# Parity of a position as an outer index, and transform tables from phases on TensorE

## The chip, the cores and the metric

One core of a Trainium2 chip runs the whole kernel. The metric is the device time of one execution in microseconds. Engines are named as in the profile: PE (TensorE), PEld (its weight loads), ACT (ScalarE), DVE (VectorE), POOL (GpSimd) and SP (SyncE, which here issues transfers). Each engine works through its own list of instructions in order; semaphores order the engines against each other.

## The reference

A state-space layer and a gated feed-forward block on the same normalised input, and all gradients of their combination. L = 2048 positions, D = 576 channels, N = 128 states, F = 4608 hidden units; inputs and outputs are bf16.

```python
def A(u):                                     # state-space layer
    dt = exp(log_dt)[:, None]
    P = exp((dt * (A_re + 1j * A_im))[:, :, None] * arange(L))
    K = einsum("dn,dnl,dn->dl", C_re + 1j * C_im, P, dt * (B_re + 1j * B_im)).real
    y = irfft(rfft(pad(u, L)) * rfft(pad(K, L)))[:L]          # causal convolution
    return y + u * Dskip
def B(x):                                     # feed-forward
    return (silu(x @ w1) * (x @ w3)) @ w2
xn = layernorm(u)
out = u + A(xn) * silu(B(xn))
# returned: out, and the vjp with grad_out for u, A_re, A_im, B_re, B_im, C_re, C_im,
# log_dt, Dskip, w1, w3, w2
```

## The kernel before, in words

The work runs in stages that overlap, each a Python generator whose steps a planner places by the times that the code gives (`self.at(...)`), with a few explicit orders (`issue_after`). The times below are those of the profile.

*Front (0 to 101 us).* The parameters are loaded, and DVE builds products of `dt` with A's parts, split into bf16 pieces `pc` that go through `PCS_dram` (L463) into the matmul operand `lhs_r`. POOL builds with iota instructions (in `selector_values`, L522) the rows `sel_dl` and `sel_val`. `early_exps` then forms on PE (through a helper, so that its line is L637) the exponents, and ACT takes 54 exponentials `E_k` of 128x1024, stored to `E_dram`. Some of these matmuls (`odd`) are followed by a second one over every other column, which adds what belongs to the odd positions. In between the layer norm (`stats`, `xn_bf`, on DVE) is computed, its transposes `xnT`, and from the normalised input and the transform's table `cCS` the early spectrum `u_e`, stored to `UH_dram` by POOL (L657). POOL also computes the products `Wr`, `Wi` of B and C.

*Kernel generation (about 101 to 340 us).* A position is l = 64a + b. The 32 values of a are split into parts whose innermost is, before the change, the parity. For each of 36 chunks of 16 channels, `kgen_chunk` takes phases on PE from `lhs_t` and the selectors `SEL` into `et_ps` (L711), their sines on ACT (`cs_k`, L713, read as 16-bit integers, so that whole turns fall off), and products with the loaded exponentials `E_l` on DVE: `p_k` (L719, stored to `PZ_dram` by SP at L722) and `q_k` (L723, to `Q_dram` at L727). `kgen_sum` multiplies `v_k` and `q_k` on PE into `kps` (L749), and POOL lays the result into the kernel's tile `KT` (L758). Between these instructions stand the matmuls of the feed-forward's hidden part (`pg`, `pu`, L1040 and L1048, with weights `wmB_w`), whose results ACT and DVE take out as `s_t`, `u_t` and `g_t` (L1058). SP also issues the loads of `E_l` (L690) and the stores of `h_t` (L1065).

At chunks 16 and 24 `dft_kernel_half` makes one half each of the tables `fT` of the kernel's transform: columns `dft_tk` on DVE, products with the row of frequencies on POOL (L812), reduction to a turn on DVE (L782 to L784), and a sine and a cosine on ACT (L816, L819), with DVE between (L817). At chunk 32 `conv_loads` stores `fT` to `TF_dram`, and SP issues eight DMA transposes of it into `iT`, the table of the inverse transform in the backward pass.

*Forward convolution and feed-forward (about 334 to 700 us).* `conv_half` transforms blocks of `KT` (`dft_block`), multiplies them with the loaded spectra and goes back. It is called for two halves of the channels.

*Backward (700 to 1731 us).* `conv_bwd_quarter`, for four quarters of the channels and up to about 1064 us, gives the gradient by the kernel and by the convolution's input. The former comes from `idft_pair` on PE (L873, with `iT`) as two position tiles at a time in `et_ps`, which ACT writes into `gk_st` with three instructions: L1341 both tiles at once, L1344 twice, scaled by the position (`lcol`). In `gk_st` the tile index t of 16 is innermost, so the two tiles t and t+1 of L1341 lie side by side (2 bytes each) and the next channel follows 32 bytes on; L1344 writes one tile. Beside this run the feed-forward's gradients (`ph` L1762, `gh` L1765, `pgw` and `gw` L1803 to L1828). Then follow the sums for the parameters (L1392 to L1400, which load `gz` from `gK_dram`) and the input gradient (`px`, L1875).

Of the kernel before, what the change touches and what calls it, by code (L numbers as in the profile page):

```python
# [10 lines left out]
ACT = mybir.ActivationFunctionType  # L11
ALU = mybir.AluOpType
AX = mybir.AxisListType
FP32 = mybir.dt.float32
BF16 = mybir.dt.bfloat16
I32 = mybir.dt.int32
I16 = mybir.dt.int16
P = 128
# [82 lines left out]
class K:  # L101
# [410 lines left out]
    def selector_values(self, st):  # L512
        nc, cfg = self.nc, self.cfg
        AV, BV, DC = cfg.AV, cfg.BV, 16
        QW, PW = DC * BV, DC * AV
        self.sel_pi = st.tile([P, 1], I32, name="pi_")
        nc.gpsimd.iota(self.sel_pi[:], pattern=[[1, 1]], base=0, channel_multiplier=1)
        self.sel_dl = dl = st.tile([P, QW + 2 * PW], BF16, name="sel_dl")
        self.sel_val = val = st.tile([P, QW + 2 * PW], BF16, name="sel_val")

        def io(out, pattern):
            nc.gpsimd.iota(out, pattern=pattern, base=0, channel_multiplier=0, allow_small_or_imprecise_dtypes=True)  # L522

        io(dl[:, 0:QW], [[1, DC], [0, BV]])
        io(val[:, 0:QW], [[0, DC], [2, BV]])
        o = QW + PW
        for k in range(2):
            io(dl[:, QW + k * PW:o + k * PW], [[4, 4], [1, 2], [2, 2], [0, AV]])
        io(val[:, QW:o], [[0, DC], [2 * BV, 2], [4 * BV, AV // 4], [0, 2]])
        io(val[0:64, o:o + PW], [[0, DC], [0, 2], [0, AV // 4], [1, 2]])  # L530
        io(val[64:P, o:o + PW], [[0, DC], [2, 2], [4, AV // 4], [0, 2]])
        return val

    def selector_rows(self, st):
# [52 lines left out]
    def conv_loads(self, after, part):  # L587
        nc, cfg = self.nc, self.cfg
        sync = Chain(self.tc, nc.sync)
        sync.prev = after  # L590
        if part == 0:
            self.skip_row = self.matp.tile([1, cfg.D], BF16, name="skip_row")
            with nc.allow_non_contiguous_dma(reason="small vector load"):
                sync.dma_start(out=self.skip_row[:].rearrange("p (g h d) -> p g h d", g=4, h=2),
                               in_=self.aps["A_Dskip"].rearrange("(o h g d) -> o g h d", o=1, h=2, g=4))
            self.CS_dram = self.dram.tile([2, 2, P, cfg.LS], BF16, name="CS_dram")
            sync.dma_start(out=self.CS_dram[:].rearrange("m i p k -> p m i k"), in_=self.cCS[:])
        elif part == 1:
            self.cT = self.matp.tile([P, 2, cfg.KT, 2 * P], BF16, name="cT")
            for m in range(2):  # L600
                for i in range(2):
                    sync.dma_start_transpose(out=self.cT[:, m, :, i * P:(i + 1) * P], in_=self.CS_dram[m, i])
        else:
            self.TF_dram = self.dram.tile([P, 2, 4, 2 * P], BF16, name="TF_dram")
            sync.dma_start(out=self.TF_dram[:], in_=self.fT[:])
            self.iT = self.matp.tile([P, 2, 2, 4, P], BF16, name="iT")
            for m in range(2):
                for i in range(4):
                    sync.dma_start_transpose(out=self.iT[:, m, :, i], in_=self.TF_dram[:, m, i])

    def early_exps(self, SELR, LR_, ep, ps):
        nc, cfg = self.nc, self.cfg
        DC = 16
        NCH = cfg.D // DC
        TW = DC * (cfg.AV + cfg.BV)
        self.e_stores, self.e_lead = [], None
        self.E_dram = self.dram.tile([NCH // 2, P, 2 * TW], BF16, name="E_dram")
        for n in range(3 * NCH // 2):
            c2, o = 2 * (n // 3), 1024 * (n % 3)
            E = ep.tile([P, 1152], BF16, name="E_k")  # L620
            self.pre(14 + 0.95 * n)
            pe = ps.tile([P, 1024], FP32, name="e_ps")
            for k in (0, 1) if n >= self.TURN else (0, 0, 1):
                ch, o1 = divmod(o + 512 * k, TW)
                odd = o1 == DC * cfg.BV
                self.lead(nc.tensor.matmul, pe[:, 512 * k:512 * k + 512], lhsT=LR_[:, c2 + ch, :], rhs=SELR[:, o1:o1 + 512],
                          start=True, stop=not odd)
                if odd:
                    self.lead(nc.tensor.matmul, pe[:, 512 * k + 1:512 * k + 512:2], lhsT=LR_[:, c2 + ch, :],
                              rhs=SELR[:, TW + 1:TW + 512:2], start=False, stop=True)  # L630
            self.S.activation(out=E[:, 0:1024], in_=pe[:], func=ACT.Exp)
            self.e_stores.append(nc.sync.dma_start(out=self.E_dram[c2 // 2, :, o:o + 1024], in_=E[:, 0:1024]))
            yield
# [25 lines left out]
    def ssm_kernel(self, T0, TK, ps, ps1):  # L659
        nc, cfg = self.nc, self.cfg  # L660
        D, N = cfg.D, cfg.N
        AV, BV = cfg.AV, cfg.BV
        DC = 16
        NCH = D // DC
        TW = DC * (AV + BV)
        GE = 6
        assert NCH % GE == 0 and AV == 2 * cfg.LT
        with self.pool(name="kg_l", bufs=2) as lp, \
# [6 lines left out]
            for ch in range(NCH):  # L675
                yield T0 + TK * ch
                self.at(T0 + TK * ch)
                if ch in (16, 24):
                    self.dft_kernel_half(dp, (ch - 16) // 8, T0 + TK * ch, TK)
                    self.at(T0 + TK * ch)  # L680
                if ch % GE == 0:
                    LT_ = lp.tile([P, GE, N], BF16, name="lhs_t")
                    nc.gpsimd.memset(LT_[:], 1.0)
# [4 lines left out]
                                                  "(k p) n -> p k n", p=DC))  # L688
                E = ep.tile([P, TW], BF16, name="E_l")
                el = self.kg_load = nc.sync.dma_start(out=E[:], in_=self.E_dram[ch // 2, :, ch % 2 * TW:(ch % 2 + 1) * TW])  # L690
                if ch in (8, 18, 32):
                    self.conv_loads(el, (8, 18, 32).index(ch))
                qv = self.kgen_chunk(ch, E, LT_[:, ch % GE, :], self.SEL, sb, qvp, ps)
                prev.append(qv)
                if ch >= 2:
# [100 lines left out]
    def dft_sines(self):  # L796
        self.turn_sines(self.S, self.cCS[:, 1], self.cCS[:, 0], self.dft_fr, self.dft_q)

    def dft_kernel_half(self, sb, i, T, TK):
        nc = self.nc  # L800
        if i == 0:
            self.fT = self.matp.tile([P, 2, 4, 2 * P], BF16, name="fT")
        sl = slice(2 * i, 2 * i + 2)
        t = sb.tile([P, 2], FP32, name="dft_tk")
        fr = sb.tile([P, 2, 2 * P], FP32, name="dft_frk")
        q = sb.tile([P, 2, 2 * P], FP32, name="dft_qk")
        for r in range(2):
            with self.tc.issue_after(self.v_last.ins):
                nc.vector.tensor_scalar(out=t[:, r:r + 1], in0=self.pcol[:], scalar1=2.0, scalar2=float(256 * i + r), op0=ALU.mult,
                                        op1=ALU.add)  # L810
        for r in range(2):
            nc.gpsimd.tensor_scalar(out=fr[:, r], in0=self.frow[:, 0:2 * P], scalar1=t[:, r:r + 1], scalar2=None, op0=ALU.mult)  # L812
        self.at(T + 0.5 * TK)
        self.wrap_turns(nc.vector, fr, q, 4.0 * self.cfg.LS)
        self.at(T + 1.5 * TK)
        nc.scalar.activation(out=self.fT[:, 1, sl], in_=fr[:], func=ACT.Sin, scale=-6.283184)  # L816
        nc.vector.scalar_tensor_tensor(out=q[:], in0=fr[:], scalar=-1.0, in1=fr[:], op0=ALU.mult, op1=ALU.max)  # L817
        self.at(T + 2.5 * TK)
        nc.scalar.activation(out=self.fT[:, 0, sl], in_=q[:], func=ACT.Sin, scale=-6.283184, bias=self.halfpi_col[:])  # L819

    def dpieces(self):
        D = self.cfg.D
# [93 lines left out]
    def conv_half(self, h, T0, TC, kp, up, rp, ypool, tp, spool, epool, ps):  # L916
# [10 lines left out]
        for b in range(NB):  # L927
            self.at(T0 + TC * 4.5 * b)
            k2 = kp.tile([P, 2, 2, KT, HW], BF16, name=f"k2_{b}")
            kr = rp.tile([P, 2, 2, KT, HW], BF16, name="kraw") if b else k2  # L930
            self.dft_block(ps, epool, lambda tt: self.KT[:, b * KT + tt, cs], kr)
            self.marks.append(self.dft_last)
            if b:
                self.shifted(k2, kr, prev, 0)
# [1 line left out]
            nc.sync.dma_start(out=self.KH2_dram[2 * h:2 * h + 2, b].rearrange("q p r k d -> p q (r k d)"),  # L936
                              in_=k2[:].rearrange("p q r k d -> p q (r k d)"))
            K2.append(k2)
        for m in range(NB):
            self.at(T0 + TC * (18, 28, 43, 65)[m])  # L940
            u = up.tile([P, 2, 2, KT, HW], BF16, name=f"u_{m}")
# [261 lines left out]
    def ssm_bwd_conv(self, T0, TQ, ps):  # L1203
# [3 lines left out]
        with self.pool(name="b_g", bufs=1, side="right") as self.bgp, \  # L1207
                self.pool(name="b_k", bufs=1, side="right") as kp, self.pool(name="b_z", bufs=2, side="right") as zp:
            self.at(T0)
            self.lcol = kp.tile([P, LT], FP32, name="lcol")  # L1210
            nc.gpsimd.iota(self.lcol[:], pattern=[[2 * P, LT // 2], [1, 2]], base=0, channel_multiplier=2,
                           allow_small_or_imprecise_dtypes=True)
            nc.vector.tensor_scalar(out=self.lcol[:], in0=self.lcol[:], scalar1=1.0 / 512, scalar2=None, op0=ALU.mult)
            self.at(T0 - 100)
# [42 lines left out]
    def conv_bwd_quarter(self, g, kp, zp, ps, T0, TQ):  # L1257
# [58 lines left out]
        for i in range(NB - 1, -1, -1):  # L1316
# [11 lines left out]
            for o, op in ((z[:, 0::3], ALU.add), (z[:, 2:0:-1], ALU.subtract)):  # L1328
                nc.vector.tensor_tensor(out=o, in0=x[:, 0::2], in1=x[:, 1::2], op=op)
            for j in range(KT // 2):  # L1330
                t = i * KT + 2 * j
                pt = ps.tile([P, 512], FP32, name="et_ps")
                pv = self.idft_pair(pt, ZZ, j)
                if t == 0:
                    gds_sb = zp.tile([1, W], BF16, name="gds_sb")
                    nc.scalar.activation(out=gds_sb[:], in_=pv[0:1, 0], func=ACT.Copy, scale=1.0 / 512)
                    with nc.allow_non_contiguous_dma(reason="small vector store"):
                        nc.sync.dma_start(out=self.aps["out_9"].rearrange("(o h g d) -> o g h d", o=1, h=2, g=4)[:, g],
                                          in_=gds_sb[:].rearrange("p (h d) -> p h d", h=2))
                sv = st[:].rearrange("p h c k d t -> p k (h c) d t")  # L1340
                nc.scalar.activation(out=sv[:, 0, :, :, t:t + 2], in_=pv.rearrange("p t (x d) -> p x d t", d=8),  # L1341
                                     func=ACT.Copy, scale=1.0 / 512)
                for k in range(2):
                    nc.scalar.activation(out=sv[:, 1, :, :, t + k], in_=pv[:, k].rearrange("p (x d) -> p x d", d=8),  # L1344
                                         func=ACT.Copy, scale=self.lcol[:, t + k:t + k + 1])
        for hf in range(2):
            for h in range(2):
                nc.sync.dma_start(out=self.gK_dram[g, :, :, h, :, hf, :],
# [707 lines left out]
```

## Time and profile before

| what | us |
|---|---|
| median of 3 runs | 1741.38 |
| lowest, highest | 1737.31, 1742.91 |
| the profiled execution, its own time | 1732.74 |
| its span in the profile | 1731.0 |
| PE busy | 1610.4 (93%) |
| DVE busy | 1396.0 (81%) |
| ACT busy | 892.9 (52%) |
| POOL busy | 486.2 (28%) |

The span runs from the first to the last instruction; the 1.7 us between it and the execution's own time lie around it. The profiled execution was faster than the three timed runs. In a group of the profile, "out<-in" are the program's tiles, then partitions x elements and type, the count, the busy time in us and the mean of one in ns, and behind the second bar the idle time of the engine just before such instructions and what ended it. In a timeline the first two numbers are the start and the duration in us, and a bracket gives the idle time before. Durations of successive instructions on ACT and PE overlap, since the next begins while the last is still writing.

### The profile page before, as it was taken

The page shows a single profiled execution, that of the slowest core. Times are in us where ns is not written, and L with a number is a line of the kernel's source. Part 1 is how long each engine was busy: PE and PEld are TensorE (multiplying, and loading weights), DVE is VectorE, ACT ScalarE, POOL GpSimd, SP SyncE. Part 2 cuts the span into 40 slices and gives each one's busy share as a digit, 9 for nine tenths or more (in the row PEclk, how much of TensorE's full clock was granted, in tenths as well). Part 3 has the DMA queues.
Part 4 walks back from the last instruction along what each step waited for, and adds up shares of the span by engine and source line. Part 5 has one row for each costly group of instructions (what it writes and reads, how often), then busy time and mean ns, then how long its engine had stood idle before and what let it go on. Part 6 is the DMA issues. An engine that isn't in the chain of part 4 may idle for free. (4 is left out here: it accounts for less than half of the span.)

```text
span 1731.0 us, 34916 instructions
## 1 busy us (share of the span) xinstructions
PE 1610.4 (93%) x13641; PEld 1182.9 (68%) x13641; DVE 1396.0 (81%) x2087; ACT 892.9 (52%) x1600; POOL 486.2 (28%) x763
## 2 busy tenths in 40 slices
PE   5999999899998999989899899999989989999998
PEld 2555454444445777878788788888877867777876
DVE  9879999797983555988986999599987965889765
ACT  5889989766652113776657676555544410001001
POOL 7456776433242111111111111111111243031132
PEclk9999999999998999999999999999999999999999
DMA  6999999888879889767585757699999999999994
GB/s 182 341 304 369 347 350 329 304 280 280 272 221 258 219 193 180 233 188 212 170 216 158 211 174 208 188 256 262 239 175 212 247 254 235 200 230 218 231 199 89
DMA packets 620779, 408.26 MB, mean 236 GB/s; under 512 B 424278, under 2 KB 562022, under 8 KB 616006
## 3 DMA queue, kind: packets, MB, share of 16 engines
q1 hardware_dynamic: 563836, 272.60, 65.0%
q0 software_dynamic: 33984, 114.33, 20.4%
q10 hardware_dynamic: 22794, 19.10, 3.9%
q8 instruction: 107, 1.75, 0.4%
q14 instruction: 58, 0.48, 0.1%
HBM read 128.52 MB, written 189.06 MB: 183 GB/s over the span
## 5 line engine op out<-in xcount | busy, mean ns | idle before, releaser
L1875 PEld LDWEIGHTS <-acts 128*128 128x128 bf16 x2304 | 226.9, 99 | 66.7 <-issue 4.7
L1826 PEld LDWEIGHTS <-xn_bf 128*128 128x128 bf16 x2304 | 225.0, 98 | 46.3 <-issue 19.3
L1397 DVE TENSOR_TENSOR pr_q<-et_ps,pz 128x1024 f32<-128x1024 f32 x144 | 175.9, 1221 | 45.9 <-PE et_ps L1392 34.5
L1811 POOL DMA_DIRECT2D out_dram<-gw x72 | 47.4, 658 | 562.4 <-ACT gw L1828 347.8
L1875 PE MATMUL px<-wT,acts 128*128 128x288 bf16 x1472 | 195.8, 292 | 4.1 <-DMA wT<-in_B_w_dram 4.1
L1040 PEld LDWEIGHTS <-xnT 128*128 128x128 bf16 x1152 | 108.2, 98 | 107.3 <-issue 22.3
L1762 PE MATMUL ph<-w2T,goT 128*128 128x256 bf16 x1440 | 171.3, 273 | 8.5 <-ACT gh L1765 8.5
L1400 DVE TENSOR_REDUCE S_all<-pr_q 128x32 f32<-128x1024 f32 x144 | 175.2, 1217 | 3.2
L1040 PE MATMUL pg<-wmB_w,xnT 128*128 128x512 bf16 x576 | 157.0, 381 | 8.8 <-DVE g_t L1058 8.6
L1040 PE MATMUL pu<-wmB_w,xnT 128*128 128x512 bf16 x576 | 157.8, 381 | 0.0
L1762 PEld LDWEIGHTS <-goT 128*128 128x128 bf16 x1440 | 139.3, 98 | 24.4 <-issue 8.4
L1803 PE MATMUL pgw<-go_o,h_n 128*128 128x288 bf16 x1152 | 152.8, 287 | 0.2 <-DVE h_n L1727 0.2
L1826 PE MATMUL pgw<-gu_n,xn_bf 128*128 128x256 bf16 x1152 | 135.3, 274 | 13.0 <-ACT gw L1807 12.2
L1826 PE MATMUL pgw<-gg_n,xn_bf 128*128 128x256 bf16 x1152 | 130.5, 273 | 1.5 <-ACT gw L1828 1.5
L1803 PEld LDWEIGHTS <-h_n 128*128 128x128 bf16 x1152 | 112.4, 98 | 28.4 <-issue 0.8
L1765 ACT CAST gh<-ph 128x512 bf16<-128x512 f32 x144 | 82.4, 606 | 75.8 <-PE ph L1762 66.9
L1054 ACT ACTIVATE s_t<-pg 128x512 bf16<-128x512 f32 x144 | 87.0, 604 | 56.7 <-PE pu L1048 42.0
L1931 ACT ACTIVATE go<-gx 128x576 bf16<-128x576 f32 x16 | 10.9, 683 | 201.1 <-DVE gx L1914 158.4
L713 ACT ACTIVATE cs_k<-et_ps 128x512 bf16<-128x512 int16 x216 | 111.0, 624 | 4.9 <-PE et_ps L711 4.8
L1875 PE MATMUL px<-wA,acts 128*128 128x288 bf16 x832 | 109.4, 288 | 2.6 <-DMA acts<-GU_dram 2.6
L758 POOL COPY KT<-k_s 64x128 bf16<-64x128 bf16 x144 | 92.0, 639 | 68.6 <-ACT k_s L755 64.0
L1059 ACT CAST u_t<-pu 128x512 bf16<-128x512 f32 x144 | 86.3, 599 | 11.5 <-PE pu L1040 11.0
(302 smaller groups left out, 3176.2 us busy)
## 6 DMA issues: line engine op xcount, KB each, us to landing
H_dram<-h_t SPq DMA_DIRECT2D x72, 256.0 KB, 5.8
U_dram<-u_t POOLq DMA_DIRECT2D x72, 256.0 KB, 4.7
G_dram<-g_t POOLq DMA_DIRECT2D x72, 256.0 KB, 4.7
Q_dram<-q_k SPq DMA_DIRECT2D x36, 512.0 KB, 5.3
gg_n<-G_dram POOLq DMA_DIRECT2D x18, 1024.0 KB, 6.0
h_n<-U_dram POOLq DMA_DIRECT2D x18, 1024.0 KB, 8.4
GG_dram<-gg_n SPq DMA_DIRECT2D x36, 512.0 KB, 6.6
GU_dram<-gu_n SPq DMA_DIRECT2D x36, 512.0 KB, 5.8
```

The lines of the kernel that those rows point to most:

```text
L713: self.sin_last = nc.scalar.activation(out=CS[:, :, o:o + 256], in_=pt[:].bitcast(I16)[:, :, 0::2], func=ACT.Sin, scale=6.283184 / 2 ** 16)
L758: nc.gpsimd.tensor_copy(out=KT[64 * hf:64 * hf + 64, :, ch // 9, h, d1:d1 + 8], in_=ks[64 * h:64 * h + 64, :, h, hf].rearrange("p d a -> p ...
L1040: ins = nc.tensor.matmul(pt[:], lhsT=xnT[:, c, ts], rhs=wm[w][:, c, :], start=(q == 0 and c == 0), stop=(q == 1 and c == nfull - 1))
L1054: nc.scalar.activation(out=s_t[:, :, q, :], in_=pgv, func=ACT.Silu)
L1059: nc.scalar.copy(out=u_t[:, :, q, :], in_=puv)
L1397: nc.vector.tensor_tensor(out=pr[:].rearrange("p r k e -> p r (k e)"), in0=T[x][:].rearrange("p z k h j a -> p (z k h j a)")[:, None].to_b ...
L1400: nc.vector.tensor_reduce(out=self.S_all[:].rearrange("p r (h c) -> p r h c", h=2)[:, :, :, d0:d0 + 2], in_=pr[:].rearrange("p r k (h j a) ...
L1762: self.pe_last = nc.tensor.matmul(ph[j][:, k, :].rearrange("p (a f) -> p a f", f=P), lhsT=lw, rhs=rh, start=(n == 0), stop=(n == nfull))
L1765: self.sc(lambda: nc.scalar.copy(out=gh[:, j], in_=ph[j][:]))
L1803: self.pe_last = nc.tensor.matmul(pgw[pi_][:, 0:pw], lhsT=hn[:, tt, fl * P:(fl + 1) * P], rhs=go_o[:, tt, po:po + pw], start=(tt == 0), st ...
L1826: self.pe_last = nc.tensor.matmul(pw_[:, 0:FG], lhsT=self.xn_bf[:, tt, c * P:(c + 1) * P], rhs=nat[:, tt, :], start=(tt == 0), stop=(tt == ...
L1875: self.pe_last = nc.tensor.matmul(px[pi_][:, 0:pw], lhsT=acts[i][:, ai, fi, :], rhs=w[:, po:po + pw], start=(n == 0), stop=(n == len(steps ...
```

## The change

Parity becomes an outer index of a: the tile order in `gk_st` and `KT` is now (parity, rest) and not (rest, parity). With it change the patterns of three iotas of `sel_val`, whose innermost run was 2 and is 8; the second matmul of `early_exps`, which took every other column and now takes every other run of 8 columns; the tile index in `dft_block`'s source, in `lcol` and in the writes to `gk_st`. There t becomes 2i+j and the second tile of a pair t+8, so that the pair of L1341 lies 16 bytes apart.

The tables `fT` are made in another way: `dft_phase_rows` writes with 26 POOL instructions the operands `ph_l` and `ph_f`, and at chunks 16, 20, 24 and 28 `dft_kernel_tile` takes two matmuls into an `et_ps` tile and one sine on ACT that reads it as 16-bit integers, as in `kgen_chunk`. `dft_kernel_half` goes. The store of `fT` and the eight transposes into `iT` move from chunk 32 into the second `conv_half` (`turn_tables`). In the order of instructions that results, the POOL instructions of `dft_phase_rows` stand after the last store of `pc` and before the products `Wr`, and the store and the transposes stand on SP about two chunks earlier than before, the transposes in two groups of four with a store of `h_t` between them. The other engines keep their order.

```diff
-        io(val[:, QW:o], [[0, DC], [2 * BV, 2], [4 * BV, AV // 4], [0, 2]])
-        io(val[0:64, o:o + PW], [[0, DC], [0, 2], [0, AV // 4], [1, 2]])
-        io(val[64:P, o:o + PW], [[0, DC], [2, 2], [4, AV // 4], [0, 2]])
+        io(val[:, QW:o], [[0, DC], [2 * BV, 2], [0, 2], [4 * BV, AV // 4]])
+        io(val[0:64, o:o + PW], [[0, DC], [0, 2], [1, 2], [0, AV // 4]])
+        io(val[64:P, o:o + PW], [[0, DC], [2, 2], [0, 2], [4, AV // 4]])
...
-                    self.lead(nc.tensor.matmul, pe[:, 512 * k + 1:512 * k + 512:2], lhsT=LR_[:, c2 + ch, :],
-                              rhs=SELR[:, TW + 1:TW + 512:2], start=False, stop=True)
+                    half = lambda ap: ap.rearrange("p (x r u) -> p x r u", r=2, u=cfg.AV // 4)[:, :, 1]
+                    self.lead(nc.tensor.matmul, half(pe[:, 512 * k:512 * k + 512]), lhsT=LR_[:, c2 + ch, :],
+                              rhs=half(SELR[:, TW:TW + 512]), start=False, stop=True)
...
-                if ch in (16, 24):
-                    self.dft_kernel_half(dp, (ch - 16) // 8, T0 + TK * ch, TK)
-                    self.at(T0 + TK * ch)
+                if ch == 10:
+                    self.dft_phase_rows(dp)
+                if ch in (16, 20, 24, 28):
+                    self.dft_kernel_tile(ps, (ch - 16) // 4)
...
-                if ch in (8, 18, 32):
-                    self.conv_loads(el, (8, 18, 32).index(ch))
+                if ch in (8, 18):
+                    self.conv_loads(el, (8, 18).index(ch))
...
+    def dft_phase_rows(self, sb):
+        nc = self.nc
+        self.ph_l = ph_l = sb.tile([P, 2, P], BF16, name="ph_l")
+        self.ph_f = ph_f = sb.tile([P, 2, 2, 2 * P], BF16, name="ph_f")
+        G = nc.gpsimd
+        def io(out, pattern, base=0):
+            G.iota(out, pattern=pattern, base=base, channel_multiplier=0, allow_small_or_imprecise_dtypes=True)
+        G.memset(ph_l[:], 0.0)
+        G.memset(ph_f[:], 0.0)
+        for k, step in ((0, 4.0), (32, 1.0)):
+            for r in range(2):
+                io(ph_l[k:k + 1, r], [[2, P]], base=r - P)
+            G.tensor_scalar(out=ph_l[k:k + 1], in0=ph_l[k:k + 1], scalar1=step / 2048, scalar2=None, op0=ALU.mult)
+        G.memset(ph_l[64:65], 1.0)
+        G.memset(ph_l[96:97], 1.0 / 16)
+        for hh in range(2):
+            for ri in range(2):
+                io(ph_f[0:1, hh, ri], [[1, 2 * P]])
+                G.memset(ph_f[32:33, hh, ri], 1.0)
+                G.memset(ph_f[64:65, hh, ri], 192.0)
+            io(ph_f[96:97, hh, 1], [[0, P // 2], [8, 2], [12, 2]] if hh else [[0, P // 2], [4, 4]], base=1 + 2 * hh)
+            G.tensor_scalar(out=ph_f[96:97, hh, 0], in0=ph_f[96:97, hh, 1], scalar1=-4.0, scalar2=None, op0=ALU.add)
+
+    def dft_kernel_tile(self, ps, i):
...
+        pt = ps.tile([P, 2, 256], FP32, name="et_ps")
+        for ri in range(2):
+            nc.tensor.matmul(pt[:, ri], lhsT=self.ph_l[:, i % 2], rhs=self.ph_f[:, i // 2, ri], start=True, stop=True)
+        nc.scalar.activation(out=self.fT[:, :, i], in_=pt[:].bitcast(I16)[:, :, 0::2], func=ACT.Sin, scale=-6.283184 / 2 ** 16)
...
-            self.dft_block(ps, epool, lambda tt: self.KT[:, b * KT + tt, cs], kr)
+            self.dft_block(ps, epool, lambda i: self.KT[:, LT // 2 * (i % 2) + 2 * b + i // 2, cs], kr)
...
+        if h:
+            self.turn_tables()
...
-            nc.gpsimd.iota(self.lcol[:], pattern=[[2 * P, LT // 2], [1, 2]], base=0, channel_multiplier=2,
+            nc.gpsimd.iota(self.lcol[:], pattern=[[1, 2], [2 * P, LT // 2]], base=0, channel_multiplier=2,
...
-                t = i * KT + 2 * j
+                t = 2 * i + j
...
-                nc.scalar.activation(out=sv[:, 0, :, :, t:t + 2], in_=pv.rearrange("p t (x d) -> p x d t", d=8),
+                nc.scalar.activation(out=sv[:, 0, :, :, t::LT // 2], in_=pv.rearrange("p t (x d) -> p x d t", d=8),
                                      func=ACT.Copy, scale=1.0 / 512)
                 for k in range(2):
-                    nc.scalar.activation(out=sv[:, 1, :, :, t + k], in_=pv[:, k].rearrange("p (x d) -> p x d", d=8),
-                                         func=ACT.Copy, scale=self.lcol[:, t + k:t + k + 1])
+                    nc.scalar.activation(out=sv[:, 1, :, :, t + k * LT // 2], in_=pv[:, k].rearrange("p (x d) -> p x d", d=8),
+                                         func=ACT.Copy, scale=self.lcol[:, t + k * LT // 2:t + k * LT // 2 + 1])
```

More of the change, by code (lines that the diff above doesn't have):

```diff
@@ L597, in conv_loads @@
             sync.dma_start(out=self.CS_dram[:].rearrange("m i p k -> p m i k"), in_=self.cCS[:])
-        elif part == 1:
+        else:
             self.cT = self.matp.tile([P, 2, cfg.KT, 2 * P], BF16, name="cT")
@@ L602, in conv_loads, with turn_tables @@
                     sync.dma_start_transpose(out=self.cT[:, m, :, i * P:(i + 1) * P], in_=self.CS_dram[m, i])
[L603 to L609, printed above, removed]
+    def turn_tables(self):
+        nc = self.nc
+        self.TF_dram = self.dram.tile([P, 2, 4, 2 * P], BF16, name="TF_dram")
+        nc.sync.dma_start(out=self.TF_dram[:], in_=self.fT[:])
+        self.iT = self.matp.tile([P, 2, 2, 4, P], BF16, name="iT")
+        for m in range(2):
+            for i in range(4):
+                nc.sync.dma_start_transpose(out=self.iT[:, m, :, i], in_=self.TF_dram[:, m, i])
     def early_exps(self, SELR, LR_, ep, ps):
@@ L797, in dft_sines @@
         self.turn_sines(self.S, self.cCS[:, 1], self.cCS[:, 0], self.dft_fr, self.dft_q)
-    def dft_kernel_half(self, sb, i, T, TK):
+    def dft_phase_rows(self, sb):
+        nc = self.nc
+        self.ph_l = ph_l = sb.tile([P, 2, P], BF16, name="ph_l")
[19 more added lines that the diff above has]
+    def dft_kernel_tile(self, ps, i):
         nc = self.nc
@@ L802, in dft_kernel_half @@
             self.fT = self.matp.tile([P, 2, 4, 2 * P], BF16, name="fT")
[L803 to L819, printed above, removed]
+        pt = ps.tile([P, 2, 256], FP32, name="et_ps")
+        for ri in range(2):
+            nc.tensor.matmul(pt[:, ri], lhsT=self.ph_l[:, i % 2], rhs=self.ph_f[:, i // 2, ri], start=True, stop=True)
+        nc.scalar.activation(out=self.fT[:, :, i], in_=pt[:].bitcast(I16)[:, :, 0::2], func=ACT.Sin, scale=-6.283184 / 2 ** 16)
     def dpieces(self):
```

## The prediction

> **What bounds the kernel now.** I read the page first, then the timelines and waits of the stages that the edit touches.
>
> ```profile
> PE 1610.4 (93%) x13641; PEld 1182.9 (68%) x13641; DVE 1396.0 (81%) x2087; ACT 892.9 (52%) x1600; POOL 486.2 (28%) x763
> PEclk9999999999998999999999999999999999999999
> ```
>
> TensorE is busy for 93% of 1731.0 us: in most places time is lost or won only where PE stands still. ACT's mean of 52% hides stages in which ACT sets the pace. The edit touches four places: the front (PE not yet fed), the kernel generation (about 101 to 340 us), the transposes at its end, and the backward convolution (700 to 1070), where the gradient of the kernel is written to `gk_st`.
>
> **Front: the index rows.** The timelines of DVE, POOL and PE, 4 to 29 us (start, duration):
>
> ```profile
> 5.01 7.58 DVE L86 CAST pc<-rho 128x640 bf16<-128x640 f32 x1
> 13.48 2.62 DVE L86 CAST pc<-sr_r 128x640 bf16<-128x640 f32 x1
> 17.00 0.49 DVE L86 CAST pc<-sr_r 128x640 bf16<-128x640 f32 x1
> 4.68 0.70 POOL L522 IOTA sel_dl<- 128x512 bf16 x1
> 5.33 10.43 POOL L522 IOTA sel_val<- 128x512 bf16 x3
> 24.87 3.81 PE L637 MATMUL e_ps<-sel_val,lhs_r 128*128 128x512 bf16 x15 [2.11 <-DMA lhs_r<-PCS_dram]
> ```
>
> The three iotas with an innermost run of 2 (256 runs) take 10.43/3 = 3.48 us each; the iota of the same size in runs of 32 (16 runs) takes 0.70. That is (3.48 - 0.70)/240 = 11.6 ns a run. With runs of 8 there are 64, so an estimated 0.70 + 48 x 0.0116 = 1.26 us (bounds 0.70 and 3.48); POOL is done 6.7 us earlier. DVE depends on it without a semaphore: one cast takes 0.49 us alone, but 7.58 and 2.62 beside the iotas. These casts feed the parameter rows that PE waits for at 24.87 through a store and a load. With the iotas ending at about 9.1, both casts are done by about 9.8 instead of 16.10: **6.3 us gained** (0, if the iotas stay, to 8.3).
>
> The accumulating second matmul of the exponents' products (`odd` in `early_exps`) becomes contiguous runs of 8:
>
> ```profile
> L637 PE MATMUL e_ps<-sel_val,lhs_r 128*128 128x512 bf16 x138 | 42.8, 386 | 6.1 <-ACT E_k L86 3.3 <-DMA lhs_r<-PCS_dram 2.1
> L637 PE MATMUL e_ps<-sel_val,lhs_r 128*128 128x256 bf16 x46 | 17.4, 379 | 0.0
> ACT E_k L86 <- PE e_ps L637: 4.8, 11, 1.6
> ```
>
> (two groups of PE, one wait of ACT.) At stride 2, 256 columns take as long as 512, which should end. ACT waited 4.8 us for these products, so that is the ceiling; ACT's own exponentials set the stage, and I take **0.7 gained** (0 to 4.8).
>
> **Front: the new phase rows.** Though called at chunk 10, the 26 POOL instructions of `dft_phase_rows` stand in POOL's order right behind the stores of `pc` (L463) and ahead of the products `Wr`, `Wi`; behind them is the spectrum's first store (L657), for which an exponential's buffer waits. Rows of POOL (timeline, then groups), DVE and ACT:
>
> ```profile
> 57.24 1.40 POOL L86 TENSOR_TENSOR Wr<-C_re_bf,B_re_bf 128x640 f32<-128x640 bf16 x1 [7.74 <-DVE Wi L86]
> 72.95 0.62 POOL L657 DMA_DIRECT2D UH_dram<-u_e  x1 [3.45 <-DVE u_e L86]
> L683 POOL MEMSET lhs_t<- 128x768 bf16 x6 | 4.4, 740 | 0.2
> L169 POOL IOTA frow<- 128x256 f32 x2 | 0.6, 342 | 0.0
> L812 POOL TENSOR_SCALAR dft_frk<-frow,dft_tk 128x256 f32<-128x256 f32 x4 | 7.3, 1826 | 0.2
> 51.62 5.52 DVE L86 TENSOR_SCALAR xn_bf<-xt,rstd,negmr 128x576 bf16<-128x576 bf16 x16
> ACT E_k L86 <- DMA UH_dram<-u_e: 0.5, 1, 0.5
> ```
>
> At these prices: the two large memsets 1.2 us (1280 elements at 740/768 ns); ten small memsets 10 x 0.25 = 2.5 by the same rate; eight iotas of at most 0.34 = 2.7; two iotas in runs of 4 and 2 (64 and 128 runs) 2 x 0.34 + 192 x 0.0116 = 2.9; four tensor_scalars between 0.25 (a memset) and 1.83 each, 1.0 to 7.3. Sum 10.3 to 16.6; I take 14, nearer the recorded tensor_scalar. The cover is POOL's 7.74 us of idle time before `Wr` and 3.45 before the first spectrum store, 11.2 in all, so 2.8 us come out behind it, and the last row shows that ACT has no slack there. The normalisation of `xn_bf` runs on DVE at the same time; if it suffers as the casts did, up to its 5.52 us comes on top, and I take 2.2. Together **5.0 lost** (0 to 16.6 - 11.2 + 5.5 = 10.9). [...]
>
> **Kernel generation: tables on PE.** Stretches of one chunk each (length; PE, PEld, DVE, ACT, POOL busy; clock), behind a wait of PE and a row of ACT:
>
> ```profile
> PE pg L1040 <- DVE g_t L1058: 8.6, 4, 2.3
> 206.79 3.05 ACT L713 ACTIVATE cs_k<-et_ps 128x512 bf16<-128x512 int16 x6
> 203.90:210.00 6.10, 6.01 (x50) 3.23 (x48) 5.35 (x10) 5.59 (x11) 5.98 (x8) 1.00 1.20 194
> 210.00:220.00 10.00, 7.69 (x50) 3.76 (x48) 8.75 (x13) 7.11 (x14) 5.76 (x8) 0.83 1.07 379
> 262.90:271.20 8.30, 5.99 (x50) 3.19 (x48) 8.27 (x13) 6.80 (x14) 4.95 (x7) 1.00 0.96 335
> 314.00:322.00 8.00, 6.06 (x50) 3.27 (x48) 5.36 (x8) 5.93 (x12) 2.49 (x6) 1.00 1.05 390
> 322.00:331.70 9.70, 7.68 (x50) 3.63 (x48) 7.15 (x11) 6.03 (x12) 3.54 (x7) 0.82 1.04 401
> ```
>
> A chunk is 50 matmuls in 6.10 us. The four long ones have the same 50 and one PE wait each. The first two hold `dft_kernel_half`, whose DVE chain and two sines sit in front of what PE needs: 3.9 + 2.2 = 6.1 us lost, part of it to the clock (0.83). That chain goes. In exchange four chunks get two matmuls of 256 columns and a sine; PE is full, so each adds what PE or ACT adds, 0.2 to 0.5 us (the sine stands in a run of its like, `cs_k`, whose six took 3.05 us): 1.3. **4.8 gained** (4.1 to 5.3).
>
> The other two come from the transposes (SP, DVE):
>
> ```profile
> 298.64 11.37 SPq L86 DMA_TRANSPOSE iT<-TF_dram  x8
> 311.74 0.62 SPq L722 DMA_DIRECT2D PZ_dram<-p_k  x1
> 317.66 0.69 DVE L719 TENSOR_TENSOR p_k<-cs_k,E_l 128x1024 bf16<-128x1024 bf16 x1 [2.61 <-DMA PZ_dram<-p_k]
> ```
>
> They hold SP for 11.37 us, the store of `p_k` goes out late, its buffer comes free late, and the chunks take 1.9 + 3.6 = 5.5 us too long. Moved into `turn_tables`, they stand two chunks earlier in SP's order, in two groups of four with a store between, and no longer beside the loads of `wmB_w`. Behind them on SP are still the stores of `p_k` and `q_k` and the next `E_l`. No row shows the hold at the new place, so its ends are all of the loss and none of it; away from the `wmB_w` loads I leave 1.0: **4.5 gained** (0 to 5.5).
>
> **Backward: the writes to `gk_st`.** The edit keeps the count of instructions, but the pair written by L1341, adjacent before (2 + 2 bytes), now lies 16 bytes apart. Timeline of ACT, then groups:
>
> ```profile
> 731.67 0.45 ACT L1341 ACTIVATE gk_st<-et_ps 128x288 bf16<-128x288 f32 x1
> 731.99 1.48 ACT L1344 ACTIVATE gk_st<-et_ps,lcol 128x144 bf16<-128x144 f32 x2
> 732.98 0.75 ACT L1341 ACTIVATE gk_st<-et_ps 128x288 bf16<-128x288 f32 x1
> 733.60 1.52 ACT L1344 ACTIVATE gk_st<-et_ps,lcol 128x144 bf16<-128x144 f32 x2
> 734.60 0.78 ACT L1341 ACTIVATE gk_st<-et_ps 128x288 bf16<-128x288 f32 x1
> L1344 ACT ACTIVATE gk_st<-et_ps,lcol 128x144 bf16<-128x144 f32 x64 | 47.9, 998 | 0.0
> L1341 ACT ACTIVATE gk_st<-et_ps 128x288 bf16<-128x288 f32 x32 | 19.4, 607 | 7.9 <-PE et_ps L873 7.9
> L1807 ACT CAST gw<-pgw 128x288 bf16<-128x288 f32 x37 | 15.5, 424 | 38.9 <-PE pgw L1803 37.9 <-DVE gx L1368 0.9
> ```
>
> L1344 writes half the elements (144, single values 32 bytes apart) and takes 998 ns; L1341 writes 288 in adjacent pairs and takes 607, and 450 where it comes first, about a contiguous cast's 424. Ends show the throughput: from L1341's end at 733.73 to the second L1344's at 735.12 is 1.39 us for 288 single values, 4.8 ns each, and L1341 itself ends 0.26 us behind its predecessor (735.12 to 735.38). So single values cost 4.3 to 5.2 ns, pairs under 1 ns an element. After the edit all 288 values of L1341 are single: 288 x 4.2 = 1.22 us against 0.27, 0.95 more, 32 times: 30.4 us of ACT. What no row shows is a 16-byte step; its ends are pairs (0 more) and the 32-byte step (0.95 to 1.2 more). I take 0.95, since each value stands alone in both. [...]
>
> How much reaches PE? The 14 stretches that hold these writes (first and sum), and PE's wait over 700 to 1075:
>
> ```profile
> 731.00:745.00 14.00, 10.76 (x114) 8.82 (x109) 11.45 (x21) 12.92 (x26) 2.17 (x4) 1.00 0.38 121
> sum 88.00, PE 73.08 PEld 62.17 DVE 77.97 ACT 74.37 POOL 9.69; mean PE 5.22 PEld 4.44 DVE 5.57 ACT 5.31 POOL 0.69
> PE ph L1762 <- ACT gh L1765: 6.9, 7, 1.3
> ```
>
> ACT has 88.00 - 74.37 = 13.6 us of idle time there against 30.4 more: at least 16.8 must spill, at most 30.4. Behind the writes on ACT's queue stand the casts `gh` and `gw`, whose PSUM buffers PE waits for already (7 waits of about 1 us). I take the middle, 23. Waits of 1.0 to 1.3 us then become about 3; after waits of 2.0 and 2.3 us two stretches above ran at 0.82 and 0.83, about 1.7 us lost each time. With 16 pairs of writes I add 4 for that (0 to 14). **27 lost** (0 to 44). I find no slack later that takes it back: the chain runs through a PE that is 93% busy.
>
> The other reindexing (`lcol`, `dft_block`, `idft`) changes no count or shape.
>
> **Sum**: 6.3 + 0.7 - 5.0 + 4.8 + 4.5 - 27 = 15.7 us slower. The profiled execution took 1732.74 us (span 1731.0) and would take 1748.4; it lies 8.6 under the median of the runs, 1741.38, so there I expect 1757.
>
> **Rivals.** (1) The 16-byte step costs nothing, and the front and the generation win 11.3: 1730, faster. For it: L1341's pairs are free now. Against it: no single-value write in the trace is cheap. It decides where L1341 grows by less than 11.3/(32 x 0.75) = 0.47 us. (2) The step costs half, or ACT's idle time swallows more: about 11 lost, 1741, no change. (3) The costs add up: POOL's rows cost 10.9 (5.9 more), the transposes still hold up `p_k` (4.5 more) and clock dips take 14 (10 more): 1777, slower.
>
> **Numbers.** Forecast 0.63; rivals 0.13, 0.12, 0.12. 0.3% (5.2 us) is about what a measurement of this kernel can tell from no change. Faster 0.14 (rival 1 and a little of 2), same 0.13, slower 0.73. The range leaves out rival 1 and the upper part of 3: 1738 to 1773.
>
> **What would show it.** Right: L1341 at about 1.5 us mean instead of 607 ns, ACT's total about 30 us higher, PE waits on `gh` and `gw` of 2 to 3 us between 730 and 1065; the three iotas in about 3.8 us, the first `pc` cast under 5; chunks without the 10.00 and 8.30. Wrong: L1341 near 0.7 us, which makes it rival 1; `Wr` starting later than its share of the earlier front, which makes the phase rows dearer.

## The result, and the profile after

| | median us | lowest, highest | runs |
|---|---|---|---|
| before | 1734.09 | 1711.57, 1756.92 | 22 |
| after | 1750.97 | 1729.02, 1765.09 | 22 |

The ratio after to before is 1.0112, with a 95% interval of 1.0075 to 1.0148: 19.4 us slower (13.0 to 25.7). The forecast was 15.7 us slower. In absolute terms it lay at 1757, because the three runs of before known then had a median 7 us above that of all 22.

The table has all runs; the ratio compares those within 1.5% of each kernel's fastest (15 of before, 13 of after), and since the profiled execution after (1757.62 us) lies above that, I read from it what happens up to the end of the convolution's gradients (about 1090 us) and leave its last stages alone.

The gradient's writes: one tile's view of `gk_st` (minimum, median, maximum ns), the timeline of ACT from 725 us (start, duration), and the groups of ACT from 700 to 1090 us.

```profile
L1362 ACT ACTIVATE gk_st<-et_ps,lcol x64: 1060/1120/1178, 726.2 to 1087.3; 128x144 bf16<-128x144 f32 x64
L1359 ACT ACTIVATE gk_st<-et_ps x32: 1423/1741/1821, 725.3 to 1085.4; 128x288 bf16<-128x288 f32 x32
...
725.29 1.46 ACT L1359 ACTIVATE gk_st<-et_ps 128x288 bf16<-128x288 f32 x1
726.25 1.74 ACT L1362 ACTIVATE gk_st<-et_ps,lcol 128x144 bf16<-128x144 f32 x2
727.50 1.78 ACT L1359 ACTIVATE gk_st<-et_ps 128x288 bf16<-128x288 f32 x1
728.78 1.78 ACT L1362 ACTIVATE gk_st<-et_ps,lcol 128x144 bf16<-128x144 f32 x2
730.04 1.79 ACT L1359 ACTIVATE gk_st<-et_ps 128x288 bf16<-128x288 f32 x1
...
L1359 ACT ACTIVATE gk_st<-et_ps 128x288 bf16<-128x288 f32 x32 | 52.0, 1624 | 9.6 <-PE et_ps L889 9.6
```

L1359 is L1341 of before. Its mean went from 607 to 1624 ns, and a group of three, which took 1.62 us from start to start before (732.98 to 734.60), takes 2.54 (727.50 to 730.04): 0.92 more, 32 times. The ends of the instructions show that a value that stands alone costs the same at 16 bytes as at 32: from one L1359's end (729.28) to the second L1362's (730.56) are 1.28 us for 288 values, from there to the next L1359's (731.83) 1.27, or 4.4 ns a value. PE's waits from 700 to 1100 us and one stretch (length; PE, PEld, DVE, ACT, POOL busy; clock) show how it gets there:

```profile
PE ph L1780 <- ACT gh L1783: 16.5, 8, 3.1
PE pgw L1844 <- ACT gw L1825: 5.4, 8, 3.5
PE et_ps L899 <- ACT gk_st L1362: 4.9, 3, 1.8
PE et_ps L889 <- ACT gk_st L1362: 4.0, 2, 2.2
725.00:740.00 15.00, 8.41 (x71) 6.61 (x70) 9.69 (x17) 14.44 (x20) 1.66 (x3) 0.82 0.35 113
```

The waits for `gh` grew from 6.9 us to 16.5 in almost as many places (7 and 8), the longest from 1.3 to 3.1; ACT is busy for 14.44 of 15 us, PE for 8.41, and the granted clock here is 0.82, where it was 1.00 in the first stretch of these writes before (731 to 745 us). The kernel before with nothing but the far pair, below, shows the same: 0.81 from 731 to 745 us. The first write starts 6.4 us earlier than before (725.3 against 731.7) and the last starts 22.0 later (1085.4 against 1063.4). So this stage alone lost 28.4 us.

The front: timelines of POOL, DVE and PE, then the matmuls that are contiguous now.

```profile
5.32 4.01 POOL L522 IOTA sel_val<- 128x512 bf16 x3
5.21 3.03 DVE L86 CAST pc<-rho 128x640 bf16<-128x640 f32 x1
9.13 0.56 DVE L86 CAST pc<-sr_r 128x640 bf16<-128x640 f32 x1
18.29 1.67 PE L640 MATMUL e_ps<-sel_val,lhs_r 128*128 128x512 bf16 x8 [1.93 <-DMA lhs_r<-PCS_dram]
L640 PE MATMUL e_ps<-sel_val,lhs_r 128*128 128x256 bf16 x46 | 12.5, 272 | 0.0
```

The three iotas take 4.01 us instead of 10.43, the two casts 3.03 and 0.56 instead of 7.58 and 2.62, and PE starts 6.6 us earlier (18.29 for 24.87). Of the phase rows, POOL's groups and timeline and a group of DVE:

```profile
43.09 0.33 POOL L812 MEMSET ph_l<- 128x256 bf16 x1
56.71 0.85 POOL L826 TENSOR_SCALAR ph_f<-ph_f 1x256 bf16<-1x256 bf16 x1
57.64 1.39 POOL L86 TENSOR_TENSOR Wr<-C_re_bf,B_re_bf 128x640 f32<-128x640 bf16 x1
L823 POOL MEMSET ph_f<- 1x256 bf16 x4 | 1.5, 374 | 0.2
L86 DVE TENSOR_SCALAR xn_bf<-xt,rstd,negmr 128x576 bf16<-128x576 bf16 x16 | 7.1, 515 | 0.0
ACT E_k L86 <- DMA UH_dram<-u_e: 2.6, 1, 2.6
```

They fill POOL from 43.09 to 57.56, so that `Wr` starts no earlier than before (57.24); `xn_bf` takes 7.06 us instead of 5.52; and ACT's wait for a spectrum store grew from 0.5 to 2.6 us. The last exponential is only 4.05 us earlier than before.

The generation, stretches of one chunk each as in the prediction, and the transposes on SP:

```profile
PE pg L1058 <- DVE g_t L1076: 2.6, 3, 1.4
206.20:212.30 6.10, 6.01 (x50) 3.22 (x48) 5.84 (x9) 5.67 (x12) 4.46 (x7) 1.00 1.05 389
255.60:261.70 6.10, 6.01 (x50) 3.22 (x48) 5.84 (x9) 5.67 (x12) 3.94 (x6) 1.00 1.00 360
292.50:299.90 7.40, 6.01 (x50) 3.27 (x48) 4.40 (x8) 5.88 (x12) 2.47 (x6) 1.00 1.02 351
306.00:313.00 7.00, 6.05 (x50) 3.26 (x48) 5.24 (x8) 5.92 (x12) 3.05 (x7) 1.00 1.05 410
278.98 5.35 SPq L611 DMA_TRANSPOSE iT<-TF_dram  x3
285.01 5.81 SPq L611 DMA_TRANSPOSE iT<-TF_dram  x4
```

The first two are the chunks that took 10.00 and 8.30 us. The other two stand behind the transposes, and are still too long.

### The profile page after: what moved, and what is told of

Read it like the earlier page. It is cut to its first block, busy times and chain, and to the rows that moved or that the text cites. A ratio compares the mean times of both kernels' runs of the same rounds, so it can differ in the third digit from the quotient of the medians.

```text
span 1755.8 us, 34939 instructions
## 1 busy us (share of the span) xinstructions
PE 1613.3 (92%) x13649; PEld 1186.7 (68%) x13649; DVE 1388.3 (79%) x2075; ACT 920.6 (52%) x1600; POOL 486.5 (28%) x785
## 5 line engine op out<-in xcount | busy, mean ns | idle before, releaser
L1780 PE MATMUL ph<-w2T,goT 128*128 128x256 bf16 x1440 | 175.9, 277 | 18.0 <-ACT gh L1783 18.0
```

The costliest lines, as they stand in the source:

```text
L1780: self.pe_last = nc.tensor.matmul(ph[j][:, k, :].rearrange("p (a f) -> p a f", f=P), lhsT=lw, rhs=rh, start=(n == 0), stop=(n == nfull))
```

## The experiments

**The write distance alone.** In the kernel before:

```diff
-  nc.scalar.activation(out=sv[:, 0, :, :, t:t + 2], ...)
+  nc.scalar.activation(out=sv[:, 0, :, :, t // 2::LT // 2], ...)
...
-  nc.scalar.activation(out=sv[:, 1, :, :, t + k], ...)
+  nc.scalar.activation(out=sv[:, 1, :, :, t // 2 + k * LT // 2], ...)
```

> The kernel before with one edit: the pair that L1341 writes lies 16 bytes apart instead of adjacent (L1344 writes to the matching places); all else, the order of instructions included, is as before. The tile order in gk_st is then not the one that the parameter sums assume, so their gradients come out permuted. Theory (write distance): the mean of L1341 rises from 607 ns to about 1600, as in the changed kernel, PE waits for gh and gw after the writes, and the whole loses 27 to 30 us, a ratio of 1.016 to 1.018. Rival (ACT's extra time is hidden, the loss of the changed kernel lies in its new order on POOL and SP): L1341 may grow, but the time stays within 3 us of before.

Measured: 1.013 of before (1.0065 to 1.0194), 22.6 us on 1735 (11.3 to 33.7, which includes the 27 to 30 expected). Its ACT and PE rows:

```profile
L1341 ACT ACTIVATE gk_st<-et_ps x32: 1426/1744/1806, 731.4 to 1090.3; 128x288 bf16<-128x288 f32 x32
PE ph L1762 <- ACT gh L1765: 16.3, 7, 3.1
```

The first write starts where it did (731.4 for 731.7), the last 26.9 us later (1090.3 for 1063.4). One access pattern, with the order of every engine unchanged, makes a loss as large as the whole one. The theory holds; the rival, that ACT's extra time is hidden, falls.

**The adjacent pair in the changed kernel.**

```diff
-  nc.scalar.activation(out=sv[:, 0, :, :, t::LT // 2], ...)
+  nc.scalar.activation(out=sv[:, 0, :, :, 2 * t:2 * t + 2], ...)
...
-  rhs=gK[:, :, :, :, d, :], ...)
+  rhs=gK[:, :, :, :, d, :].rearrange("p z k f (u r) -> p (z k f) r u", r=2), ...)
...
```

> The changed kernel with one edit: the pair of L1359 is written side by side again (tile index 2u + parity in gk_st), and the matmuls of the parameter sums (L1410) read their moving operand with a stride of two values to restore the order. Theory (write distance): L1359 is back at about 0.6 us, the 29 us are gone, and what the front and the kernel generation won stays: 11 to 12 us faster than before, a ratio of about 0.993. Rival 1 (the loss is not the write distance): the time stays near that of the changed kernel, 1.011. Rival 2 (strided reads on PE cost like strided writes on ACT): L1359 is cheap, but L1410's 576 matmuls grow from 1070 us on and take back 10 us or more.

Measured: 0.9958 of before (0.9924 to 0.9991), 1725.57 us. The tile's view, and the matmuls of the parameter sums:

```profile
L1359 ACT ACTIVATE gk_st<-et_ps x32: 407/728/783, 723.7 to 1056.1; 128x288 bf16<-128x288 f32 x32
L1410 PE MATMUL et_ps<-gz,qT x576: 216/217/312, 1119.6 to 1692.9; 128*128 128x128 bf16 x192
```

The writes are as cheap as before (median 728 ns; 733 in the kernel before), and the strided read costs PE nothing (median 217 ns; 219 in the kernel before). The loss is gone. The win is 7.3 us (1.6 to 13.2), less than the 11 to 12 expected, which the interval does not exclude; the next section looks for the rest.

**All writes in runs of eight.**

```diff
-  st = self.bgp.tile([P, 2, D // 64, 2, 8, LT], BF16, name="gk_st")
+  st = self.bgp.tile([P, 2, D // 64, 2, LT, 8], BF16, name="gk_st")
...
-  rhs=gK[:, :, :, :, d, :], start=True, stop=True)
+  rhs=gK[:, :, :, :, :, d], start=True, stop=True)
...
```

> The changed kernel with gk_st and gz laid out with the 8 channels innermost, so that all three writes of a group are runs of 8 adjacent values (16 bytes); the matmuls of the parameter sums read one value in 16 bytes. Theory (write distance): L1359 at about 0.42 us and L1362 at about 0.28 us, ACT's busy time about 85 us lower than in the changed kernel, and in the stretches of the writes PE waits less than before the change: 11 to 25 us faster than before, a ratio of 0.985 to 0.993. Rival (the read distance costs PE what the write distance cost ACT): L1410 grows to twice its time or more, and the kernel is slower than with the pair layout.

Measured: 1.0287 of before (1.0242 to 1.0333): the rival. The writes, the reads, and who waits for these matmuls:

```profile
L1362 ACT ACTIVATE gk_st<-et_ps,lcol x64: 356/383/473, 727.4 to 1051.5; 128x144 bf16<-128x144 f32 x64
L1359 ACT ACTIVATE gk_st<-et_ps x32: 383/412/483, 727.1 to 1050.9; 128x288 bf16<-128x288 f32 x32
L1410 PE MATMUL et_ps<-gz,qT x576: 386/405/409, 1114.4 to 1753.0; 128*128 128x128 bf16 x192
...
  DVE pr_q L1415: 90.7, 43
```

L1359 now takes what the contiguous cast of 288 values took (412 ns, 424), L1362 falls from 1120 to 383, and PE's waits for `gh` between them are gone; but PE reads one value in 16 bytes, its matmul goes from 219 to 405 ns 576 times, and DVE waits 90.7 us for it (34.5 before). The price of the distance has moved from the writer to the reader, where it is paid more often.

**The phase rows spread.** Three of the 26 POOL instructions behind the copies into `KT` of each chunk:

```diff
-  if ch == 10:
-      self.dft_phase_rows(dp)
+  if ch == 5:
+      rows = self.dft_phase_rows(dp)          # now yields behind each instruction
+  if 5 <= ch < 15:
+      for _ in range(3):
+          with self.tc.issue_after(self.kt_last.ins):
+              next(rows, None)
```

> The changed kernel with the 26 POOL instructions of dft_phase_rows spread over chunks 5 to 13, three behind each chunk's copies into KT, instead of in one block in the front; the order on the other engines is unchanged. Theory (the block delays xn_bf on DVE and the first spectrum stores): the last exponential, 4.05 us earlier than before in the changed kernel, comes 6.6 to 7.2 us earlier, xn_bf takes 5.5 us again and not 7.06, and all of it stays until the end of the kernel generation, since POOL has about 2 us of idle time a chunk there: 3 us less than the changed kernel, which the runs can hardly tell and the trace can. Rival (POOL in the generation is no free place): the copies into KT or the stores of u_t come late and chunks grow beyond 6.12 us.

Measured: 1.0112 (1.0054 to 1.0171), as expected not to be told from the changed kernel. By the trace the last exponential is 8.20 us earlier than before (4.05 in the changed kernel), and the first product of the generation 8.20 (4.05); it stays at that until the tables. The normalisation's row:

```profile
L86 DVE TENSOR_SCALAR xn_bf<-xt,rstd,negmr x16: 419/423/429, 45.3 to 50.4; 128x576 bf16<-128x576 bf16 x16
```

It is back at 423 ns each, as before; no chunk grew for good (one of 6.30 us is followed by one of 5.94). By this pair of traces the block cost 4.2 us, more than expected here and nearer to the prediction's 5.0. More traces make it less: the last exponential starts at 82.0, 81.5 and 81.4 us in the three kernels with the block (the changed one and the two experiments above) and at 77.9, 78.3 and 79.0 in the three without it (this one and the last two below), 3.2 us apart by their means.

**What distance costs.** In the kernel before, the pair 4 and 8 bytes apart:

```diff
+  f0 = 4 * (t // 2 // 2) + t // 2 % 2                       # 8 bytes: 8 * (t // 2 // 4) + t // 2 % 4
-  nc.scalar.activation(out=sv[:, 0, :, :, t:t + 2], ...)
+  nc.scalar.activation(out=sv[:, 0, :, :, f0:f0 + 3:2], ...)   # 8 bytes: f0:f0 + 5:4
...
```

> The kernel before with the two values that L1341 writes in one step 4 bytes apart (not adjacent, but in the same 16 bytes; the tile order in gk_st is not the sums'). Theory A (a write is cheap when the one before it fell into the same 16 bytes): L1341 stays at about 607 ns mean. Theory B (a write is cheap only if two adjacent values fill one 4-byte word): L1341 is at about 1600 ns, as at 16 bytes.

> As before it, with the two values 8 bytes apart, still in the same 16 bytes. Theory A: L1341 at about 607 ns mean. Theory B: about 1600 ns. If the price grew with the distance (theory C), 4 bytes would lie nearest to the adjacent pair, 8 bytes between it and the 1600 ns of 16 bytes.

The first fence is 4 bytes, the second 8:

```profile
L1342 ACT ACTIVATE gk_st<-et_ps x32: 759/1078/1144, 735.7 to 1073.4; 128x288 bf16<-128x288 f32 x32
737.28 1.12 ACT L1342 ACTIVATE gk_st<-et_ps 128x288 bf16<-128x288 f32 x1
739.14 1.13 ACT L1342 ACTIVATE gk_st<-et_ps 128x288 bf16<-128x288 f32 x1
```

```profile
L1342 ACT ACTIVATE gk_st<-et_ps x32: 770/1076/1157, 734.0 to 1074.2; 128x288 bf16<-128x288 f32 x32
735.51 1.12 ACT L1342 ACTIVATE gk_st<-et_ps 128x288 bf16<-128x288 f32 x1
737.39 1.11 ACT L1342 ACTIVATE gk_st<-et_ps 128x288 bf16<-128x288 f32 x1
```

All three theories fall. 4 and 8 bytes cost the same (medians 1078 and 1076 ns), which rules out C, and lie between the adjacent pair (733) and 16 bytes (1744). A group takes 1.62 us from start to start with adjacent values, 1.86 at 4 bytes (737.28 to 739.14), 1.88 at 8 (735.51 to 737.39), 2.54 at 16. Two steps, then: about 0.25 us more per 144 pairs when the pair is not adjacent, and 0.67 on top at 16 bytes. (Whether it is a border every 16 bytes or the distance that makes the second step was not tried: no kernel has a nearer pair on both sides of such a border.) The total times, one run each, were 1739.54 and 1738.75 us; before ran from 1716.70 to 1763.67 beside them, so they say nothing of the 8 us that 32 steps of 0.25 make.

**Both repairs, and the transposes spread.** The second adds to the first one transpose behind each store to `KH2_dram`:

```diff
-  if h:
-      self.turn_tables()
+  with self.tc.issue_after(kh.ins):            # kh: the store of block b to KH2_dram
+      self.turn_tables(4 * h + b)              # one transpose of eight
```

> The changed kernel with both repairs: adjacent pairs in gk_st (as in e2_near_in_after) and the phase rows spread over the generation (as in e4_rows_spread). Theory (the two costs add): the generation ends about 17 us earlier than before, of which some 4 to 6 us go to transfers at the start of the feed-forward's output, and the whole is 9 to 13 us faster than before, a ratio of 0.9925 to 0.995. Rival (the output stage waits for its loads whatever comes ahead of it): no faster than e2_near_in_after, 0.996, with longer waits for hcC, hcA and w2g.

> As e7_near_rows, with one of the eight transposes of fT behind each of the eight stores to KH2_dram in the two halves of the convolution, instead of two groups of four in the last chunks of the generation. Theory (SP's hold delays the stores of p_k): the last chunks take 6.1 us each, the generation ends another 2 to 4 us earlier, and the whole is up to 3 us faster than e7_near_rows. Rival: the transposes now hold up the stores of h_t and the loads of hcA, and the output stage waits longer by as much or more.

Measured: 0.9892 (0.9821 to 0.9963) and 0.9887 (0.9828 to 0.9946), medians 1716.79 and 1714.41. Both beat both kernels, and that of before by some 19 us of 1739 (6 to 31). That is more than the 9 to 13 expected of the first, whose interval includes these and just reaches the rival's 0.996. Between the two the runs tell nothing. By the trace the generation ends 14.3 and 17.7 us earlier than before (17 was expected of the first), so the spread transposes give 3.4 us, as expected: in the second kernel every chunk from the 30th on takes 6.12 us. At the first write of `gk_st` 9.0 and 10.7 us are left, and 9.0 and 10.4 at the last. The rest of the 19 lies behind that and is not explained: from the last write to the end, four traces of one and the same sequence of instructions (before, the far pair, 4 and 8 bytes) take from 655 to 668 us. PE's waits from 480 to 600 us in the second:

```profile
PE ptr L1232 <- DVE go_o L1195: 7.6, 5, 6.5
PE po L1178 <- DMA hcC<-H_dram: 2.6, 1, 2.6
PE po L1178 <- DMA w2g<-in_B_w_dram: 1.9, 1, 1.9
PE po L1178 <- DMA hcA<-H_dram: 0.2, 1, 0.2
```

## Why the prediction was right, point by point

*Index rows.* Estimated 1.26 us an iota, measured 4.01/3 = 1.34; 6.3 us earlier forecast, 6.6 measured at PE's first product. The chain from POOL through DVE's casts, with no semaphore between the two, was read rightly: beside the shorter iotas the two casts took 3.03 and 0.56 us, beside the longer ones 7.58 and 2.62, and one alone 0.49.

*Contiguous matmuls.* 379 became 272 ns, and the exponentials gained another 0.5 us by the 32nd (7.1 against 6.6): 0.7 forecast.

*Phase rows.* A block of 14 us forecast, 14.5 measured, by errors that cancel: the tensor_scalar on one partition took 0.85 us and not 1.83, the small memsets 0.37 and not 0.25. The loss of 5.0 is 4.2 by the spread kernel (3.2 by the means of six traces), and both places were named: `xn_bf` (2.2 forecast, 1.5 measured) and the spectrum's store (2.8 forecast; ACT's wait grew by 2.1). The upper end for `xn_bf`, its whole 5.5 us on top, did not come.

*Tables.* The long chunks went, 3.9 + 2.2 = 6.1 us as read; each of the four new tiles costs 0.22, so 5.2 net against 4.8. But the 6.1 was one trace's: the kernels with the far pair and with the 8 bytes have the instructions of before here and lose 4.4 and 4.5. All three wait for `g_t` for the same 2.3 us, but only before's clock falls behind that wait (0.83; 1.00 in the other two). In before itself the second wait of 2.31 us, in the chunk of 8.30, is followed by a clock of 1.00. That part of the loss comes and goes.

*Transposes.* This term was mis-sized: 4.5 forecast, 3.0 measured (the generation's lead grew from 9.28 us ahead of them to 12.25 at the end). I left 1.0 of the loss; two chunks of 7.40 and 7.00 us, 1.3 and 0.9 too long, stayed. Spread, they gave 5.4 (12.29 to 17.71), nearly all of the 5.5 at stake. Here too one trace is a rough measure: from chunk 30 to the last product of the generation the four kernels with before's order take 42.2, 40.3, 42.0 and 40.1 us, three with the order after 39.3, 38.9 and 38.1, and the one with spread transposes 36.8. By the means the move gained 2.4 of 4.4 us at stake.

*Writes.* 0.95 us each forecast, 0.92 measured; 27 us lost forecast, 26.9 with the one edit and 28.4 in the changed kernel. The mechanism was right; that the sizes met so closely was in part luck. The 0.95 comes from 4.2 ns a value, where the prediction's own row gives 4.8 (1.12 us) and its bounds begin at 4.3. The three quarters of ACT's extra time that I let through, and the clock's part, were chosen between bounds and fit as a sum; no run separates them.

*What the sum left out.* I let the gains of the front and the generation run through to the end. They shrink: the changed kernel is 12.25 us ahead at the generation's end and 6.4 at the first write of `gk_st`, and other kernels show the same (13.1 to 8.0 with the near pair, 14.0 to 4.6 with the channels inside, 14.3 to 9.0 and 17.7 to 10.7 in the last two). By how much is known only roughly. The four kernels that are as before up to there start that write at 731.7, 731.4, 735.7 and 734.0 us, the three that are as after at 725.3, 723.7 and 727.1. By the means a lead of 11.7 us becomes one of 7.8. Between lies the start of the feed-forward's output. PE's waits there for `hcC`, `hcA`, `w2g` and `go_o`, the longest of each in before and after:

```profile
544.18 3.54 PE L1145 MATMUL po<-w2a,hcC 128*128 128x288 bf16 x14 [4.61 <-DMA hcC<-H_dram]
```

```profile
526.34 1.09 PE L1163 MATMUL po<-w2g,hcA 128*128 128x288 bf16 x4 [2.51 <-DMA w2g<-in_B_w_dram]
534.47 1.89 PE L1163 MATMUL po<-w2a,hcC 128*128 128x288 bf16 x14 [0.91 <-DMA hcC<-H_dram]
546.25 4.09 PE L1163 MATMUL po<-w2a,hcA 128*128 128x288 bf16 x32 [1.78 <-DMA hcA<-H_dram]
555.11 0.86 PE L1217 MATMUL ptr<-ident_bf,go_o 128*128 128x128 bf16 x5 [3.91 <-DVE go_o L1180]
```

In all, PE waited for these four from 480 to 600 us for 6.4 us before, and for 8.1, 11.1 and 8.7 in the three kernels that are as before up to there; for 10.2 after, and for 9.7 and 12.4 in the two that are as after; and for 12.3 in the last kernel above. So these waits grow with the lead, but they differ as much among equal kernels, and the kernel with the rows spread, with 14.5 us of lead at the generation's end, shows only 7.5. That they take the 4 us is likely and not shown, and what these loads and `go_o` wait for in turn stays open. I had read before's wait of 4.6 us for `hcC` as a cost that stays the same. The interval of the result, 13.0 to 25.7 us, holds the forecast of 15.7, so the runs do not show this in the sum; but some 4 us of gain that I counted are not there.

The rivals: the first (the 16-byte step is free) was the opposite of what came, the second and third did not occur; the transposes did stall again, as the third said, but for 2.2 us and not 5.5.

## What to carry to other kernels

Reindexing a tile is not free because the count of instructions stays: ask for every write and read of it how far apart successive elements now lie, and price that from the nearest row that has such a pattern already. Here the far pair alone cost 22.6 us (11.3 to 33.7), and L1344 next to L1341 held the answer. An engine that is busy for half of the span can be the bound in the stretches that count (ACT: 52% of the span, 14.44 of the 15 us from 725 on in the changed kernel), so its slack is to be read there, and a gain far ahead need not reach the end: here a mean lead of 11.7 us at the end of the generation was one of 7.8 at the first write of `gk_st`. A wait or a lead read off one trace is worth a second trace of the same instructions; here equal instructions reached the same point up to 4 us apart.

## What the runs showed of the hardware

ACT's writes of bf16 to SBUF had three prices here: adjacent pairs at contiguous speed (L1341 from 403 ns for 288 values; the contiguous cast of 288 took 424); pairs 4 or 8 bytes apart about 0.25 us more per 144 pairs, 1.7 ns a pair; pairs 16 bytes apart 0.92 us more, 6.4 ns a pair. In the changed kernel values alone cost 4.4 ns each at 16 and at 32 bytes. PE read its moving operand at a stride of 4 bytes for nothing (217 against 219 ns for 128 columns) and at 16 bytes at almost twice the time (405). POOL's iota was priced by its innermost runs: 3.48 us for 256 runs, 1.34 for 64, 0.70 for 16, all of 512 elements, which is 11 to 13 ns for each further run. And of four waits of PE for `g_t` in the kernel before, of 2.31, 2.31, 1.94 and 2.02 us, the first and the last were in stretches of 10.00 and 9.70 us with a granted clock of 0.83 and 0.82 (0.50 and 0.81 in the two parts of the first that followed the wait), the other two in stretches with 1.00.
